# Output copies that read with a stride and write in sequence, decay tables over two queues, and a new fixed order of the opening, in a fused attention and MLP kernel

## The chip, the cores and the metric

The kernel runs on one core of one Trainium2 chip. The metric is the time of one execution on the device, in microseconds (us). A kernel is called faster or slower only if the difference is over 2%.

The engines are written PE (TensorE, matmuls), PEld (its weight loads), DVE (VectorE), ACT (ScalarE), POOL (GpSimd) and SP (SyncE, which here only starts transfers). A profile's span is about 1.75 us shorter than the time of the same execution (222.3 us and 224.09 before). Each execution also comes with the mean clock that was granted to TensorE, as a share of full speed.

## The reference, cut to what matters

The kernel computes a block-wise linear attention with decay, followed by an MLP with a periodic activation. There are 4 batches, 8 heads, 768 tokens and head size 64.

```python
def _attn_ref(q, k, v, lam):                    # cut
    for b in range(nb):                         # blocks of 64 tokens
        intra = einsum('bhic,bhjc->bhij', qb, kb) * Dmask      # lam ** (i - j), causal
        intra = einsum('bhij,bhjd->bhid', intra, vb)
        inter = einsum('bhid,bhde->bhie', qb * lam_pow, kv_state)
        out[:, :, sl] = intra + inter
        kv_state = lam_block * kv_state + einsum('bhsd,bhse->bhde', kb * rev_pow, vb)

def _moe_ref(x, w_in, w_out, alpha):            # x: 3072 x 512, w_in: 512 x 2048, w_out: 2048 x 512
    h = x @ w_in
    s = np.sin(alpha * h)
    g = h + s * s / (alpha + 1e-09)
    return g @ w_out
```

## The kernel before

The kernel works in blocks of 128 tokens, so attention has 24 steps (six for each batch). Four steps make one chunk of 512 tokens for the MLP, and there are six chunks. For each chunk the MLP has 16 "A" groups (w_in, then sine on ACT, square on POOL, DVE or ACT, and the sum `gT` on DVE) and 16 "B" groups (w_out). PE has by far the most work (busy 209.8 of 222.3 us; DVE 152.1, ACT 139.2), so the question is always when PE has to wait.

All operations are recorded first. A small list scheduler in the program then places them in an order for each engine, by assumed durations. Three strings or tables steer it: `LOADS` (the order of the transfers that SP starts), `SCRIPT` (the order of the work on PE) and, after the change only, `ENG` (operations that must run on a given engine). The item `w1` in `SCRIPT` is a filler: a matmul on zeros whose result nobody reads, there to keep PE busy.

For the first steps, q is loaded in rows of 1 KB (four tokens of 64 values), not of 256 bytes. The tokens of such a block arrive permuted: what lies at `g * 4 + t` in order lies at `t * 32 + g` here. The permutation is undone where the attention output is copied from PSUM into `xT`, the MLP's input:

```python
            x_out, x_in = xT[x][:, :, col:col + 128], dst      # dst: PSUM, fp32; xT: SBUF, bf16
            if s < NPQ:                                        # NPQ = 10: the permuted steps
                x_in = dst.rearrange("p a (t g) -> p a t g", g=32)
                x_out = bass.AP(xT[x], col, [[NKC * TCH, 128], [TCH, NKC], [1, 4], [4, 32]])
            rec((("ACT", 0.59), ("DVE", 0.66)), lambda e, name: copy_of(e, name, x_out, x_in), ...)
```

This reads PSUM in sequence and writes bf16 with a step of four elements (8 bytes). The decay tables come from `lam` in two small transfers, both started by ACT. The table `Lk` scales k, and the table `L4` scales permuted q:

```python
            rec("ACT", lambda e: e.dma_start(lam_bc[:, :], ...), 0.5, writes=["lam"], prio=-1)
            ...                                                # lnlam, lnL, Lq
            rec("ACT", lambda e: e.activation(Lk[:, :, :], lnL[:, :, :], ACTF.Exp, scale=-1.0), 0.3,
                reads=["lnL"], writes=["Lk"])
            rec("ACT", lambda e: e.dma_start(lam4_sb[:, :], lam4), 0.5, writes=["lam4"], prio=-2)
            rec("ACT", lambda e: e.activation(lnlam4[:, :], lam4_sb[:, :], ACTF.Ln), 0.3,
                reads=["lam4", "table"], writes=["lnlam4"], prio=-1)
            ...                                                # L4
```

A lower `prio` goes first on its engine, so `lam4` is started before `lam_bc`. The profile leaves numbers out of names: what it calls `lam_sb` is `lam4_sb`.

## Time and profile before

| | time, us | span, us | granted clock |
|---|---|---|---|
| three timed runs | 221.70, 221.84, 222.15 (median 221.84) | not listed | not listed |
| the profiled run | 224.09 | 222.3 | 0.985 |

The page of the kernel before, its head and three rows of the table of 40 slices (5.6 us each; a digit is a share in tenths, 9 is 90% or more):

```profile
span 222.3 us, 3797 instructions
...
PE   7586899899999999999999999999999999999994
...
PEclk9889699999999999999999999999999999999999
DMA  5999999999999899999899998440002110011123
```

PE is busy from the ninth slice on. The clock is below full in slices 2, 3 and 5, with a low of 0.6 in the fifth (22 to 28 us). The DMA engines are nearly full until about 140 us (8 or 9 in the slices from 5.6 us on).

The clock's row tells nothing of the first microseconds. Its record begins at 6.07 us here, and what comes before is counted as full speed. The weight loads of the fillers at the start are 0.43 us apart, though, where matmuls of the same width later start 0.216 us apart:

```profile
3.73 0.15 PEld L773 LDWEIGHTS m_ps<-zeros,ident 128*128 128x128 bf16 x1 [0.28 <-issue]
4.16 0.15 PEld L773 LDWEIGHTS m_ps<-zeros,ident 128*128 128x128 bf16 x1 [0.28 <-issue]
```

"Full clock" and "no stretch" below mean after this opening.

The same by windows:

```profile
core 0: us, PE busy (x) PEld busy (x) DVE busy (x) ACT busy (x) POOL busy (x), PEclk, DMA share, GB/s
...
24.00:28.00 4.00, 4.00 (x19) 1.72 (x19) 1.67 (x4) 1.50 (x4) 0.00 (x0) 0.68 1.17 298
...
36.00:44.00 8.00, 6.94 (x50) 3.01 (x48) 7.66 (x12) 7.71 (x14) 6.02 (x7) 1.00 1.05 341
...
60.00:200.00 140.00, 140.00 (x991) 67.33 (x991) 106.21 (x158) 97.11 (x161) 44.67 (x45) 1.00 0.68 135
```

From 60 to 200 us PE has no gap at all. What can be won lies before 60 us. In 24 to 28 us PE is busy throughout, but at a granted clock of 0.68. In 36 to 44 us it stands idle for 1.06 us.

The timeline of the opening (start, duration, engine, line, what; in brackets the idle time before it and what ended it). The first MLP group is the last line:

```profile
6.28 0.24 ACT L492 ACTIVATE Lk<-lnL 128x48 f32<-128x48 f32 x1 [0.27 <-DVE lnL L488]
...
19.94 1.29 ACT L550 CAST xT<-m_ps 128x512 bf16<-128x512 f32 x1 [0.36 <-PE m_ps L656]
...
21.25 0.37 ACT L550 CAST Zs<-Z_ps 64x256 bf16<-64x256 f32 x1
...
21.67 0.40 PE L652 MATMUL m_ps<-qkT,Zs 128*128 128x128 bf16 x4 [1.32 <-ACT Zs L550]
22.45 1.30 ACT L550 CAST xT<-m_ps 128x512 bf16<-128x512 f32 x1 [0.84 <-PE m_ps L656]
...
23.90 1.86 PE L701 MATMUL m_ps<-xT,w 128*128 128x512 bf16 x4 [1.04 <-ACT xT L550]
```

The copy of 1.29 us at 19.94 holds ACT until 21.23. Only then does ACT copy the attention state `Zs` that step 3 waits for, and step 3's own copy of 1.30 us stands directly before the first group. The group's four matmuls take 1.86 us. In the groups of instructions of the first 60 us, such a copy is:

```profile
L550 ACT CAST xT<-m_ps 128x512 bf16<-128x512 f32 x7 | 9.1, 1302 | 8.7 <-PE m_ps L656 8.7
```

### The profile page before, as it was taken

Reading aid. Unit: us, or ns where it says so; the run is one execution under the profiler, and the core shown is the slowest. Engines: PE = TensorE matmul, PEld = TensorE weight load, DVE = VectorE, ACT = ScalarE, POOL = GpSimd, SP = SyncE. Lnnn points to the kernel's source line nnn. Section 1 sums busy time; section 2 is a strip of 40 time slices with the busy share of each in tenths; the row PEclk is TensorE's granted clock in tenths of the full one; section 3 lists DMA queues with packets and bytes.
Section 4 is the critical chain, followed back from the end, with each engine's and each line's share of the span. In section 5 each row is a group of like instructions: output and inputs, shape, how many; then the busy total and the mean of one; then the engine's idle time right before and its main releaser. Section 6 shows DMA issues by size and latency. Waiting matters only on the chain.

```text
span 222.3 us, 3797 instructions
## 1 busy us (share of the span) xinstructions
PE 209.8 (94%) x1512; PEld 102.6 (46%) x1512; DVE 152.1 (68%) x227; ACT 139.2 (63%) x226; POOL 69.6 (31%) x79
## 2 busy tenths in 40 slices
PE   7586899899999999999999999999999999999994
PEld 2354344445445554444445445444454444444453
DVE  3786589996569997488887947698581788751010
ACT  3458599943888885678974356897655676640111
POOL 4251099740058921254745422311000011000000
PEclk9889699999999999999999999999999999999999
DMA  5999999999999899999899998440002110011123
GB/s 112 283 230 324 302 326 350 330 325 255 225 253 166 152 220 189 270 214 250 173 198 228 231 195 186 129 50 1 0 3 94 47 47 3 0 47 47 47 97 142
DMA packets 92322, 37.49 MB, mean 169 GB/s; under 512 B 80384, under 2 KB 87312, under 8 KB 92304
## 3 DMA queue, kind: packets, MB, share of 16 engines
q1 hardware_dynamic: 88528, 31.07, 65.3%
q10 hardware_dynamic: 3776, 6.18, 8.0%
q8 instruction: 12, 0.20, 0.4%
q14 instruction: 6, 0.05, 0.1%
HBM read 27.28 MB, written 6.29 MB: 151 GB/s over the span
## 4 chain that ended last, share of the span: by engine, by line
PE 84%; DVE 7%; ACT 4%; DMA 2%; issue 0%; SPq 0%; DVEq 0%
PE m_ps L701 36%; PE m_ps L732 35%; PE A_ps L630 3%; ACT xT L550 3%; DMA k<-in_k_dram 2%; DVE S_m L634 2%; PE m_ps L656 2%; PE m_ps L754 2%; PE A_ps L656 1%; PE m_ps L652 1%; DVE gT L716 1%; DVE qk L578 1%; DVE u L713 1%; PE m_ps L609 1%; PE Z_ps L676 1%; PE A_ps L652 1%
## 5 line engine op out<-in xcount | busy, mean ns | idle before, releaser
L701 PE MATMUL m_ps<-xT,w 128*128 128x512 bf16 x384 | 92.9, 383 | 2.3 <-ACT xT L550 1.4
L732 PE MATMUL m_ps<-w,gT 128*128 128x512 bf16 x368 | 87.2, 379 | 0.0
L707 ACT ACTIVATE t<-m_ps,alpha_sb 128x512 bf16<-128x512 f32 x96 | 64.9, 687 | 32.3 <-PE m_ps L701 31.6
L716 DVE SCALAR_TENSOR_TENSOR gT<-u,r_sb,m_ps 128x512 bf16<-128x512 bf16 x96 | 69.2, 741 | 9.8 <-POOL u L713 6.0
L713 POOL TENSOR_TENSOR u<-t 128x512 bf16<-128x512 bf16 x26 | 27.8, 1074 | 92.3 <-ACT t L707 92.1
L701 PEld LDWEIGHTS m_ps<-xT,w 128*128 128x128 bf16 x384 | 35.8, 98 | 45.1 <-issue 2.7
L732 PEld LDWEIGHTS m_ps<-w,gT 128*128 128x128 bf16 x368 | 34.7, 98 | 40.7 <-issue 0.7
L713 DVE TENSOR_TENSOR u<-t 128x512 bf16<-128x512 bf16 x36 | 18.4, 512 | 20.7 <-ACT t L707 20.7
L550 ACT COPY osb<-m_ps 128x512 f32<-128x512 f32 x18 | 10.6, 586 | 21.3 <-PE m_ps L732 21.2
L712 ACT ACTIVATE u<-t 128x512 bf16<-128x512 bf16 x34 | 21.3, 629 | 0.8
L550 ACT CAST xT<-m_ps 128x512 bf16<-128x512 f32 x14 | 13.9, 995 | 12.5 <-PE m_ps L656 12.5
L572 POOL TENSOR_TENSOR qk<-k,Lk 128x512 bf16<-128x512 f32 x16 | 18.1, 1137 | 11.3 <-DMA k<-in_k_dram 7.3
L634 DVE TENSOR_TENSOR S_m<-A_ps,mask 128x1024 bf16<-128x1024 f32 x14 | 17.1, 1220 | 2.1 <-PE A_ps L630 2.0
L550 DVE COPY osb<-m_ps 128x512 f32<-128x512 f32 x5 | 3.4, 689 | 17.1 <-DMA out_dram<-osb 14.5
L634 DVE TENSOR_TENSOR S_m<-A_ps,maskP 128x1024 bf16<-128x1024 f32 x10 | 12.2, 1220 | 1.8 <-PE A_ps L630 1.7
L550 DVE CAST Zs<-Z_ps 64x256 bf16<-64x256 f32 x17 | 7.1, 419 | 6.7 <-PE Z_ps L676 6.5
L581 POOL TENSOR_TENSOR qk<-q,Lq 128x512 bf16<-128x512 f32 x9 | 10.1, 1119 | 3.9 <-DMA q<-in_q_dram 3.8
L630 PE MATMUL A_ps<-qkT 64*128 64x128 bf16 x192 | 9.8, 222 | 1.4 <-DVE S_m L634 1.3
L773 PE MATMUL m_ps<-zeros,ident 128*128 128x512 bf16 x23 | 9.4, 528 | 1.6 <-POOL ident L514 1.6
L550 ACT CAST v<-v 128x512 bf16<-128x512 f32 x15 | 9.3, 622 | 2.2 <-DMA v<-in_v_dram 2.2
L630 PEld LDWEIGHTS A_ps<-qkT 64*128 64x128 bf16 x192 | 5.6, 95 | 9.8 <-issue 3.9
L550 ACT CAST Zs<-Z_ps 64x256 bf16<-64x256 f32 x23 | 8.6, 374 | 0.2
(71 smaller groups left out, 130.5 us busy)
## 6 DMA issues: line engine op xcount, KB each, us to landing
k<-in_k_dram SPq DMA_DIRECT2D x24, 256.0 KB, 5.3
q<-in_q_dram SPq DMA_DIRECT2D x24, 256.0 KB, 5.1
v<-in_v_dram SPq DMA_DIRECT2D x24, 256.0 KB, 5.1
out_dram<-osb ACTq DMA_DIRECT2D x23, 256.0 KB, 2.1
wst<-in_moe_w_in_dram SPq DMA_DIRECT2D x8, 512.0 KB, 7.0
wst<-in_moe_w_out_dram SPq DMA_DIRECT2D x8, 512.0 KB, 5.7
qkT<-qk SPq DMA_TRANSPOSE x14, 3.9
out_dram<-osb ACTq DMA_DIRECT2D x1, 128.0 KB, 1.7
```

What stands on the lines that cost most here:

```text
L550: return e.copy(out_ap, in_ap) if name == "ACT" else e.tensor_copy(out_ap, in_ap)
L572: rec(two, lambda e, _: e.tensor_tensor(k2[c], k32[r][:, :, :], Lk_b, ALU.mult), reads=[f"k32.{r}", "Lk"], writes=[f"k2.{c}"], tag=f"k{s}")
L581: rec(two, lambda e, _: e.tensor_tensor(q2[c], q32[r][:, :, :], Lq_b, ALU.mult), reads=[f"q32.{r}", "Lq"], writes=[f"q2.{c}"], tag=f"q{s}")
L630: last = e.matmul(A_ps[:, 4 * h + jp, :], qkT[j][rows, 4 + jp, :], qT(s, rows, jp))
L634: rec("DVE", lambda e: e.tensor_tensor(S_m[j2][:, :, :], A_ps[:, :, :], mask_b, ALU.mult), 1.22, reads=["S0", "S1", "maskP" if s < NPQ els ...
L701: last = e.matmul(m_ps[i][:, 0:n], w1[:, kc, 128 * m:128 * (m + 1)], xT[x][:, kc, 0:n], start=(kc == 0), stop=(kc == NKC - 1))
L707: rec("ACT", lambda e: e.activation(t16[tt][:, 0:n], m_ps[i][:, 0:n], ACTF.Sin, scale=alpha_sb[:, m:m + 1]), 0.27 + 0.41 * f, reads=[f"m.{ ...
L712: return e.activation(u16[tt][:, 0:n], t16[tt][:, 0:n], ACTF.Square)
L713: return e.tensor_tensor(u16[tt][:, 0:n], t16[tt][:, 0:n], t16[tt][:, 0:n], ALU.mult)
L716: rec("DVE", lambda e: e.scalar_tensor_tensor(out=gT[g][:, m, 0:n], in0=u16[tt][:, 0:n], scalar=r_sb[:, m:m + 1], in1=m_ps[i][:, 0:n], op0 ...
L732: last = e.matmul(m_ps[bank][:, :], gT[g][:, m, 128 * s4:128 * (s4 + 1)], w2[:, m, :], start=(m == 0), stop=(m == NM - 1))
L773: last = e.matmul(m_ps[bank][:, :], ident[:, :], zeros[:, :])
```

## The change

The intent is to shorten the opening. The copies into `xT` are turned round: they read PSUM with a stride and write in sequence. The two `lam` transfers are started by two engines. The order of loads and matmuls and the engines of 56 operations were found by a search. One step fewer is permuted (`NPQ` 9). The penalty in the scheduler's model is an assumption of the program. The middle of the long strings and tables is cut.

```diff
-    "k0 k1 k2 q0 q1 v0 q2 k3 q3 k4 v1 v2 v3 w0 q4 w1 w2 q5 k5 w3 v4 w4 w5 w6 q6 k6 w7 ...
+    "k0 q0 v0 k1 q1 k2 q2 k3 q3 v1 v2 q4 v3 w0 k4 w1 q5 w2 w3 w4 w5 k5 w6 w7 w8 w9 v4 ...
-    "t0 w1 t1 w1 S0 a t2 w1 S1 o0 t3 w1 S2 o1 S3 w1 w1 o2 w1 o3 w1 A0.0 w1 A0.1 T4 A0.2 ...
+    "T0 w1 w1 w1 S0 t1 w1 w1 w1 a w1 S1 t2 w1 o0 S2 t3 w1 o1 S3 w1 o2 w1 w1 w1 o3 A0.0 ...
-NPQ, NW, FETCH = 10, 5, 1.2
+NPQ, NW, FETCH = 9, 5, 1.2
+ENG = {"k0": "DVE", "k1": "DVE", "k2": "POOL", ..., "zs8.1": "ACT"}
@@ in the scheduler: a fixed engine is taken from ENG; its model of time
@@ has a queue for POOL's transfers and a penalty where DVE and POOL overlap
-            rec("POOL", lambda e: e.memset(zeros[:, :], 0.0), 0.5, writes=["zeros"])
+            rec("DVE", lambda e: e.memset(zeros[:, :], 0.0), 0.3, writes=["zeros"], prio=-1)
-                rec("ACT", lambda e: e.dma_start(lam4_sb[:, :], lam4), 0.5,
+                rec("POOL", lambda e: e.dma_start(lam4_sb[:, :], lam4), 0.8,
                     writes=["lam4"], slot="lam4", work=0.05, prio=-2)
             if s < NPQ:
-                x_in = dst.rearrange("p a (t g) -> p a t g", g=32)
-                x_out = bass.AP(xT[x], col, [[NKC * TCH, 128], [TCH, NKC], [1, 4], [4, 32]])
+                x_in = dst.rearrange("p a (t g) -> p a g t", g=32)
+                x_out = x_out.rearrange("p a (g t) -> p a g t", t=4)
```

## The prediction

> **What bounds the kernel now.** By windows, TensorE (PE) is busy without a gap from 60 to 200 us, and that work is fixed. What can be won lies before 60 us. (a) The first MLP group starts at 23.9 us (timeline). (b) It runs its first 2.5 us at half speed: matmuls of 512 columns start 430 ns apart, later 216; the granted clock in 24 to 28 us is 0.68. (c) PE stands idle 1.06 us in 36-44 and 0.47 us in 44-60. The end (2.8 us after PE's last matmul) is not touched.
>
> The opening's chain: tables (Lk ready at 6.5 us, though k0 landed at 3.9), key and query scaling on VectorE (DVE), first transposes at 9.4, four masks of 1.22 us, copies into xT on ScalarE (ACT). Copies of permuted steps take 1.30 us, those of later steps 0.58 (ACT) or 0.69 (DVE), same shape. They delay ACT directly: the state copy that attention step 3 waits for stood behind xT's copy until 21.25.
>
> A second limit lies close: the load queue. DMA share is 0.99 or more per window from 8 to 150 us; loads land one after another, 1.1 to 1.2 us each for k, q, v and 1.5 to 2 us per weight block. The last weight block landed at 52.2 us, v7 (needed for the second chunk) at 53.4; the second chunk's first matmul began at 59.9.
>
> **What the change does.**
> - xT copies: written in sequence, read from PSUM with stride. I expect about 0.6 us on ACT, 0.7 on DVE: 0.6 to 0.7 saved on each of 9. No such strided PSUM read is in the trace. [...]
> - Two lam loads in parallel: lam_bc goes first on ACT and should land near 4.1 instead of 5.8 us, so key scaling starts near 5. [...]
> - q0 and v0 come right after k0: first transposes near 7, not 9.4.
> - Fixed engines, new order: balance only.
>
> **How much counts.** The order still brings v3 13th and w0 14th: by the old landings v3 near 17.4, w0 near 19.1. After its cast (1.1 us) the first group can start near 20.3: 3.6 us earlier. But weight blocks then come at about PE's pace, so part returns as waits for weights; v7 keeps landing near 54, so the second chunk can't start before about 55.5. I expect 56 to 57, with one left-over block of chunk 0 behind it, not two. Net gain about 3.8 us: 221.84 to **218.1 us**, range 216.4 to 219.8. Faster by over 2%: 0.32; within 2%: 0.67; slower: 0.01.
>
> **To check.** Permuted xT copies 0.55 to 0.75 us; Lk by 5.2; first transposes at 6.6 to 7.6; first group at 19.8 to 21.3; second chunk at 55.5 to 57.5; DMA still full; no gaps from 60 us on.
>
> **What would make it wrong.** Strided PSUM reads as slow as the strided writes (then 219 to 220); the half-speed stretch falling elsewhere (1.7 us either way); loads flowing faster once buffers come free sooner (then 216); new waits past 60 us from the new order.

## The result, and the profile after

Ratios in this document are the mean time of one kernel's fast runs over that of the other's fast runs of the same rounds, so they are not quite the ratio of the medians quoted beside them. "Fast" runs are those within 1.5% of the fastest of the same kernel.

| | median, us | all runs, us |
|---|---|---|
| before | 221.77 | 221.32, 221.70, 221.84, 222.15 |
| after | 220.43 | 220.25, 220.36, 220.49, 220.64 |

The ratio is 0.9941 (95% interval 0.992 to 0.9962), which is "same" at 2%. The gain is 1.3 us, where 3.7 us had been forecast (221.84 to 218.1). The measured time lies outside the forecast range of 216.4 to 219.8.

The page after. The profiled execution took 220.64 us, at a granted clock of 1.0:

```profile
span 218.9 us, 3772 instructions
...
PE   5786997999999999999999999999999999999995
...
PEclk9999999999999999999999999999999999999999
DMA  4999999999999999998999999241101110012023
```

```profile
core 0: us, PE busy (x) PEld busy (x) DVE busy (x) ACT busy (x) POOL busy (x), PEclk, DMA share, GB/s
...
24.00:28.00 4.00, 3.87 (x28) 1.74 (x26) 3.60 (x6) 3.48 (x7) 2.08 (x2) 1.00 1.11 344
...
36.00:44.00 8.00, 5.99 (x51) 2.93 (x51) 6.46 (x9) 5.87 (x10) 5.53 (x7) 1.00 1.07 337
...
60.00:200.00 140.00, 138.05 (x963) 66.72 (x980) 103.23 (x155) 95.93 (x162) 33.73 (x34) 1.00 0.68 139
```

The spans of the two profiles differ by 3.4 us (222.3 and 218.9), close to what was forecast. The times of the two kernels differ by 1.3 us. Both are right: the two executions of before that one compares with are not alike. The half speed is gone from the profile after. The last window must be read with care. It holds 963 matmuls but 980 weight loads, where before had 991 of each, so 17 matmul records are missing from the trace (25 of the 752 large matmuls in the whole run). At about 0.2 us each they can account for the 1.95 us that PE seems to stand idle.

The timeline of the opening after, with the same events:

```profile
6.10 0.20 ACT L576 ACTIVATE lnlam<-lam_sb 128x2 f32<-128x2 f32 x1 [1.94 <-DMA lam_sb<-in_lam_dram]
6.40 0.52 ACT L579 ACTIVATE L<-E_f,lnlam 128x24 f32<-128x24 f32 x2
6.82 0.23 ACT L561 ACTIVATE Lk<-lnL 128x48 f32<-128x48 f32 x1
...
20.54 1.04 POOL L619 CAST w<-wst 128x1024 bf16<-128x1024 f32 x1 [2.64 <-DMA wst<-in_moe_w_in_dram]
20.67 0.58 ACT L619 CAST xT<-m_ps 128x512 bf16<-128x512 f32 x1 [1.16 <-PE m_ps L725]
...
21.63 1.04 PE L770 MATMUL m_ps<-xT,w 128*128 128x512 bf16 x4 [0.88 <-POOL w L619]
```

The copy takes 0.58 us. The first group starts 2.27 us earlier, and its four matmuls take 1.04 us where they took 1.86. What it waits for has changed: `xT` is ready at 21.25, but the first weight block only lands at 20.48 and is cast until 21.58. `Lk` comes no earlier: it ends at 7.05 us, where it had ended at 6.52. ACT's fixed order puts the tables of `lam_sb` before it, and `lam_sb` lands last.

The groups of the first 60 us: the copies after the change, on both engines.

```profile
L619 DVE CAST xT<-m_ps 128x512 bf16<-128x512 f32 x3 | 2.1, 688 | 0.1
...
L619 ACT CAST xT<-m_ps 128x512 bf16<-128x512 f32 x3 | 1.8, 585 | 3.1 <-PE m_ps L725 3.1
```

The chain of waits after, for 27 to 40 us (start, length, what):

```profile
27.05 8.23 DMA wst<-in_moe_w_in_dram
...
35.33 1.04 POOL w L619
36.37 1.01 POOL u L782
...
37.40 2.08 DVE gT L785 x3
39.48 0.59 PE m_ps L801 x2
```

A weight block lands at 35.27. POOL casts it, and only then squares one group's sine, and DVE builds three `gT` behind that. PE waits for them twice, 1.62 and 0.23 us. This is a new wait, and it begins with a transfer. It is where part of the earlier start is given back: idle time in 36 to 44 us rose from 1.06 to 2.01 us (0.16 us of it, at 42.2 us, may be a missing record).

### The profile page after: what moved, and what is told of

It is laid out like the page before. It is cut to its first block, busy times and chain, and to the rows that moved or that the text cites. A ratio compares the mean times of both kernels' runs of the same rounds, so it can differ in the third digit from the quotient of the medians.

```text
span 218.9 us, 3772 instructions
## 1 busy us (share of the span) xinstructions
PE 204.8 (94%) x1483; PEld 101.4 (46%) x1510; DVE 148.9 (68%) x227; ACT 136.5 (62%) x232; POOL 63.0 (29%) x73
## 4 chain that ended last, share of the span: by engine, by line
PE 81%; DMA 7%; SPq 6%; DVE 2%; issue 2%; POOL 1%
PE m_ps L801 37%; PE m_ps L770 33%; DMA wst<-in_moe_w_in_dram 7%; SPq L543 6%; PE A_ps L699 3%; PE A_ps L725 2%; PE m_ps L823 2%; DVE gT L785 2%; PE m_ps L725 1%; PE A_ps L721 1%; POOL w L619 1%; PE Z_ps L745 1%; PE m_ps L721 1%; POOL u L782 0%; PE A_ps L681 0%
## 5 line engine op out<-in xcount | busy, mean ns | idle before, releaser
L770 PE MATMUL m_ps<-xT,w 128*128 128x512 bf16 x369 | 90.0, 379 | 4.3 <-DVE gT L785 1.8
L781 ACT ACTIVATE u<-t 128x512 bf16<-128x512 bf16 x45 | 28.1, 629 | 1.2
L703 DVE TENSOR_TENSOR S_m<-A_ps,mask 128x1024 bf16<-128x1024 f32 x15 | 18.3, 1222 | 6.4 <-PE A_ps L699 6.1
L782 POOL TENSOR_TENSOR u<-t 128x512 bf16<-128x512 bf16 x11 | 11.4, 1039 | 25.1 <-ACT t L776 25.1
L641 POOL TENSOR_TENSOR qk<-k,Lk 128x512 bf16<-128x512 f32 x11 | 12.2, 1111 | 16.7 <-DMA k<-in_k_dram 14.3
L650 POOL TENSOR_TENSOR qk<-q,Lq 128x512 bf16<-128x512 f32 x11 | 13.2, 1203 | 9.1 <-DMA q<-in_q_dram 8.8
L641 DVE TENSOR_TENSOR qk<-k,Lk 128x512 bf16<-128x512 f32 x13 | 10.5, 810 | 3.5 <-ACT Lk L561 2.7
L619 ACT CAST Zs<-Z_ps 64x256 bf16<-64x256 f32 x27 | 9.8, 365 | 4.5 <-PE Z_ps L745 2.9
L647 POOL TENSOR_TENSOR qk<-q,L 128x512 bf16<-128x512 f32 x8 | 8.8, 1111 | 9.4 <-DMA q<-in_q_dram 6.0
L619 POOL CAST w<-wst 128x1024 bf16<-128x1024 f32 x9 | 9.3, 1038 | 7.5 <-DMA wst<-in_moe_w_in_dram 7.5
```

Source lines behind the costliest of these rows:

```text
L619: return e.copy(out_ap, in_ap) if name == "ACT" else e.tensor_copy(out_ap, in_ap)
L641: rec(two, lambda e, _: e.tensor_tensor(k2[c], k32[r][:, :, :], Lk_b, ALU.mult), reads=[f"k32.{r}", "Lk"], writes=[f"k2.{c}"], tag=f"k{s}")
L650: rec(two, lambda e, _: e.tensor_tensor(q2[c], q32[r][:, :, :], Lq_b, ALU.mult), reads=[f"q32.{r}", "Lq"], writes=[f"q2.{c}"], tag=f"q{s}")
L703: rec("DVE", lambda e: e.tensor_tensor(S_m[j2][:, :, :], A_ps[:, :, :], mask_b, ALU.mult), 1.22, reads=["S0", "S1", "maskP" if s < NPQ els ...
L770: last = e.matmul(m_ps[i][:, 0:n], w1[:, kc, 128 * m:128 * (m + 1)], xT[x][:, kc, 0:n], start=(kc == 0), stop=(kc == NKC - 1))
L781: return e.activation(u16[tt][:, 0:n], t16[tt][:, 0:n], ACTF.Square)
```

## The experiments

Two theories were set against each other at the start. The first says that the strided-read copies carry the gain, and that the tables and the search add nothing. The second says that every part contributes, and that the gain is lost later, at the load queue. A third question, why the profiles showed 3.4 us and the times 1.3, was put to runs as well.

Eighteen runs were made, some of one kernel twice, each beside runs of the kernel before on the same chip. Unless a run is said to be wrong, its result agreed with the reference.

### The copies alone, the rest alone, and before once more

`x_only` is the kernel before with the copies' new form and nothing else. `x_undo` is the kernel after with the copies' old form. Together they split the change in two.

```diff
 # x_only, on the kernel before                     # x_undo is the reverse, on the kernel after
-                x_in = dst.rearrange("p a (t g) -> p a t g", g=32)
-                x_out = bass.AP(xT[x], col, [[NKC * TCH, 128], [TCH, NKC], [1, 4], [4, 32]])
+                x_in = dst.rearrange("p a (t g) -> p a g t", g=32)
+                x_out = x_out.rearrange("p a (g t) -> p a g t", t=4)
```

`before_again` has no edit.

> The kernel before, unchanged, to see whether its first profile stands for its timed runs. Theory A: the half-speed stretch at 23 to 27 us (granted clock 0.985 over the span) belonged to that one profiled execution (224.1 us); the timed runs (221.3 to 222.2) did not have it. Then spans here are about 220.0 us at clock 1.00 for most runs, and the first MLP group runs its matmuls 216 ns apart from the start. Rival B: every run has the stretch; then clock 0.985 in each and spans near 222.

> The kernel before with the strided-read copies into xT alone; order of all engines the same. Theory (copies stand on the chain to the first group): copies fall from 1.30 to about 0.6 us, the state copy before step 3 no longer waits, first group about 1.5 to 2.5 us earlier than in the kernel before, time down by 1 to 2 us. Rival (loads bind): copies fall, but the time falls by less than 0.7 us, since the weight blocks land when they did.

> The kernel after with strided writes into xT again, same order. If the copies carry the gain: 1 us or more slower than after, that is back at the kernel before or worse (ratio 1.000 or above). If the order carries it: ratio stays near 0.995.

| same chip | median, us | runs, us | ratio to before (95%) |
|---|---|---|---|
| before, 8 runs | 223.78 | 221.14 to 226.26 | |
| before_again, 2 runs | 224.17 | 222.62, 225.72 | 1.0107 (0.9928 to 1.0287) |
| x_only | 220.41 | 219.76 to 220.75 | 0.9928 (0.9873 to 0.9983) |
| x_undo | 221.82 | 221.54 to 222.08 | 1.0001 (0.9961 to 1.0041) |

The copies alone gain as much as the whole change. The rest alone gains nothing against the fast runs of before. That ratio leaves out four of the eight runs of before, the slower ones, and the section on the clock below comes back to them.

The groups of `x_undo`, first 60 us, show that DVE suffers from strided writes as ACT does, so that the copies' cost belongs to the form and not to the engine (the strided reads took 585 ns on ACT and 688 on DVE in the groups above; in the later steps of before, copies that read and write in sequence take 584 and 691):

```profile
L619 DVE CAST xT<-m_ps 128x512 bf16<-128x512 f32 x3 | 3.9, 1303 | 0.1
L619 ACT CAST xT<-m_ps 128x512 bf16<-128x512 f32 x3 | 3.9, 1302 | 2.2 <-PE m_ps L725 2.2
```

`x_only` did what its theory said in time (1.5 us at full clock, see below), but its first group came only 1.2 us earlier (22.71 us), not 1.5 to 2.5. Neither expectation of `before_again` held: its profiled run had the half speed at the first group again (0.985, 225.72 us), its other run less of it (0.992), and one of the eight runs beside it had none.

The unexpected finding is the width of before: 5 us between its fastest and slowest run on one chip (eight runs), where `x_only` spreads over 1.0 and `x_undo` over 0.5 (four runs each).

### The tables, one queue or two, and cheap loads

`lam_undo` is the kernel after with both `lam` transfers started by ACT, `lam_sb` first, as before. `lam_early` keeps one queue too, but starts `lam_bc` first and makes `Lk` before the tables of `lam_sb`. In both, `q0` is pinned to POOL so that all other orders stay as they are after the change. `cheap_kv` is the kernel after with k and v of the first nine steps loaded in 1 KB rows too. Its tokens are then in the wrong places and its result is wrong (relative error 0.81). It asks what the load queue costs. (In the profile of before, the q loads in 1 KB rows that landed at 8.95, 11.14 and 13.06 us came 0.83 to 0.89 us after the load ahead of them, and the k and v loads at 12.23, 14.26, 15.48 and 16.66 us 1.08 to 1.21 us.)

```diff
 # lam_undo, on the kernel after
-                rec("POOL", lambda e: e.dma_start(lam4_sb[:, :], lam4), 0.8,
+                rec("ACT", lambda e: e.dma_start(lam4_sb[:, :], lam4), 0.5,
 # lam_early: the same, and
-                    writes=["lam4"], slot="lam4", work=0.05, prio=-2)
+                    writes=["lam4"], slot="lam4", work=0.05, prio=-1)
-                reads=["lnL"], writes=["Lk"])
+                reads=["lnL"], writes=["Lk"], prio=-2)
-                    reads=["lam4", "table"], writes=["lnlam4"], prio=-1)
+                    reads=["lam4", "table", "Lk"], writes=["lnlam4"], prio=-1)
 # cheap_kv, on the kernel after, for k and v
+                if s < NPQ:
+                    a = bass.AP(src.tensor, ..., [[4 * D, 32], [2 * S * D, 4], [S * D, 2], [1, 4 * D]])
+                    d = bass.AP(dst[r], 0, [[H * D, 128], [4 * D, 2], [1, 4 * D]])
```

> The kernel after with both lam loads on ScalarE's queue again, the per-step table first as in the kernel before; nothing else moves but three small instructions. Theory (in the kernel after the table path got worse, Lk at 7.05 against 6.52, because its second load from GpSimd landed at 6.1 us and ScalarE's order puts Lk behind it, but it binds nothing): Lk near 6.5, first transposes about 0.5 us earlier, first group within 0.3 us of 21.6, time within 0.3 us of after. Rival (the opening's chain from the tables binds): 0.5 us faster than after.

> Both lam loads on ScalarE's queue, lam_bc first, and Lk made before the other table. Lk should be ready near 4.7 us instead of 7.05, the other table near 6. First transposes then wait for q0 (lands at 6.8) and come near 8.0 instead of 8.8. Theory (loads bind the first group): it still starts at 21.3 to 21.7, time within 0.4 us of after. Rival (tables bind): first group 0.8 us or more earlier, time near 219.6.

> Wrong result on purpose: k and v of the first 9 steps are fetched in rows of 1 KB as q is, same bytes and same buffers but the wrong tokens, so each of these loads should take about 0.8 instead of 1.2 us. Order of all engines as in after. Theory (the load queue binds the opening): w0 lands about 2.5 to 3 us earlier, w15 and v7 about 5 us earlier, first group near 20 us (then the attention chain binds), waits for weights at 36 to 39 us go, time 1.5 to 3 us below after. Rival (chains on the engines bind): time within 0.5 us of after.

| same chip | median, us | Lk ends | first group of chunk 0 | first group of chunk 1 |
|---|---|---|---|---|
| lam_undo | 220.11 | 8.22 | 21.76 | 56.58 |
| lam_early | 220.06 | 4.28 | 21.46 | 56.96 |
| cheap_kv | 217.90 | | 22.23 | 56.09 |

In this table and those below, the start of chunk 1 is that of its first weight load; its first matmul follows within 0.22 us. The timelines of `lam_undo` and, below it, of `lam_early`:

```profile
4.39 0.20 ACT L577 ACTIVATE lnlam<-lam_sb 128x2 f32<-128x2 f32 x1 [1.08 <-DMA lam_sb<-in_lam_dram]
...
7.98 0.24 ACT L562 ACTIVATE Lk<-lnL 128x48 f32<-128x48 f32 x1 [1.11 <-DVE lnL L558]
```

```profile
4.04 0.24 ACT L562 ACTIVATE Lk<-lnL 128x48 f32<-128x48 f32 x1 [0.27 <-DVE lnL L558]
5.81 0.20 ACT L577 ACTIVATE lnlam<-lam_sb 128x2 f32<-128x2 f32 x1 [1.40 <-DMA lam_sb<-in_lam_dram]
```

The order of ACT's work moves `Lk` by 3.9 us and the time by 0.05 us. (`lam_undo` was expected to bring `Lk` near 6.5; it came at 8.22, since `lam_bc` landed at 6.63 us, where it had landed at 5.77 in before, and DVE then took 1.05 us for `lnL`, not 0.21.) One transfer's table comes early and the other's late in either case, and the first transposes need both. In the order after the change, the tables are not what bounds.

The later of the two `lam` transfers landed at 5.77 us (before, both on ACT), 6.08 (after, on POOL), 5.79 (`lam_early`, both on ACT) and 6.63 us (`lam_undo`, both on ACT). The second queue brought no gain here. (`lam_sb` is the later one after the change and in `lam_early`, `lam_bc` in the other two.)

Cheaper loads gained 2.2 us against `lam_undo`, although the first group started 0.5 us later and not near 20 us, as had been expected. The last weight block landed at 47.79 us, where it landed at 52.19 in `lam_undo` and at 53.27 in the profile after. So in the order after the change, the stream of loads does bind. (k, v and weights all land earlier in this run, so it does not tell them apart.) The windows say where, first `lam_undo` and then `cheap_kv`, with the columns of the windows shown before:

```profile
20.00:44.00 24.00, 22.26 (x158) 10.59 (x158) 20.21 (x31) 19.34 (x32) 15.23 (x16) 1.00 1.11 342
```

```profile
20.00:44.00 24.00, 23.03 (x164) 11.02 (x163) 21.32 (x32) 19.50 (x33) 16.28 (x15) 1.00 1.01 343
```

PE is busy 0.77 us longer in these 24 us. That is a part of the 2.2 us. The rest was not traced to single waits.

### The clock

The profile of before has two stretches at half speed after the opening, 9.48 to 12.89 and 23.13 to 26.55 us, 3.413 us each, with a granted clock of 0.50 throughout. The second lies on the first MLP group. `before_warm` has 6 fillers where before has 1, in the two places ahead of the first group, to see whether they keep that stretch away. `before_p2` and `before_p3` are before unedited, to see more profiles of it. `x_cold` is `x_only` with four fillers cut to 16 columns, so that PE is less busy there (its expectation says five; the edit and the trace have four).

```diff
 # before_warm, on the kernel before; the scheduler is still told of one
-    ... S3 w1 w1 o2 w1 o3 w1 A0.0 ...
+    ... S3 w1 w1 o2 w6 o3 w6 A0.0 ...
 # x_cold, on x_only; an f1 is a filler of 16 columns
-    ... S3 w1 w1 o2 w1 o3 w1 A0.0 ...
+    ... S3 f1 f1 o2 f1 o3 f1 A0.0 ...
```

> The kernel before with 10 more warm-up matmuls in the idle time of TensorE before the first group (6 instead of 1 in two places), order otherwise the same. Theory (the kernel before is slow in some runs, 223 to 226 us, because TensorE's clock was halved for 3.4 us from about 23 us on after the idle time at 20.5 to 23.9): no half-speed stretch at the first group, all runs at 221 to 221.8 us, and the first group's start unchanged at 23.8 to 24.0. Rival (the spread has another cause): runs of 223 us and more appear as before.

> The kernel before once more, for one more profile. Theory (its slow runs of 223 us and more have TensorE's clock halved for one 3.4 us window at the first group; its runs below 222.5 do not): if this execution is above 223 us, two half-speed windows, the second near 23 us; if below 222.6, no window there. Rival: the time and the window don't go together.

> As before_p2, another execution of the kernel before; the same test of time against window.

> The kernel before with strided-read copies (as x_only) and the five filler matmuls before the first group cut to 16 columns, so that TensorE does 1 us less in 18.7 to 22.7 us; orders unchanged. Theory: the half-speed window at the first group comes back in many runs, as in the kernel before, and those runs are 1.5 to 2.5 us longer than x_only's 219.7 to 220.8; the first group's start stays at 22.6. Rival (the window costs nothing): time as x_only in all runs.

| | median or time, us | half-speed stretches in the profile, us |
|---|---|---|
| before_warm | 222.49 (221.82 to 223.94) | 10.12 to 13.53 |
| before_p2 | 223.48, one run | 11.52 to 18.35 |
| before_p3 | 224.19, one run | 9.81 to 13.22, 23.46 to 26.87 |
| x_cold | 221.95 (219.87 to 223.32) | 11.16 to 17.99, 21.40 to 24.81 |

The ratio of `before_warm` to before is 0.9974 (0.9916 to 1.0032), that of `x_cold` 0.9883 (0.9788 to 0.9977). `before_p3` came out as expected. `before_p2` did not: it is above 223 us and has twice 3.41 us of half speed, but none near 23 us. `before_warm` missed too: all its runs lie above 221.8 us, and its first group started at 23.38 us and not at 23.8 to 24.0.

By themselves these ratios decide nothing. What tells more is the granted clock of every single execution. One stretch of 3.413 us at half speed lowers the mean over 221 us by 0.5 x 3.413 / 221 = 0.0077. So I count 0.992 as one such stretch, 0.985 as two, and 0.977 as three. For runs without a profile this is an estimate; the profiles bear it out (`x_only` 0.992 with one, before 0.985 with two, `x_cold` 0.977 with three, two of them in one stretch of twice the length). The 44 runs of before that stood beside other runs, on five chips, sort like this (the two of `before_again`, `before_p2` and `before_p3` are not counted: one had one stretch and three had two):

| half-speed stretches (granted clock) | before: runs, median us | after: runs, median us | x_only | x_early (below) |
|---|---|---|---|---|
| none (0.998 to 1.0) | 7, 221.73 | 11, 220.25 | 4, 220.25 | 5, 219.68 |
| one (0.991, 0.992) | 16, 223.06 | 5, 221.31 | 6, 219.76 | 5, 219.75 |
| two (0.983 to 0.985) | 13, 224.33 | none | none | none |
| three (0.977) | 8, 224.04 | none | none | none |

Four of the 11 runs of after in the first row are those of the first result. That is the answer to the third question. Before runs in several states of the clock, and its median rises by about 1.3 us with each of the first two stretches. The order none, one, two holds within each of the five chips too, as far as the states occurred, with steps of 0.9 to 2.2 us between medians of one to five runs. Single runs overlap: 220.85 to 222.45 us with none, 221.32 to 223.93 with one, 222.95 to 225.27 with two. Six runs of the last two rows are slow by the rule of 1.5%; without them their medians are 224.21 and 224.01. The profile that the prediction read is a run with two. At two stretches against none, before and after differ by 224.33 - 220.25 = 4.1 us, about what was forecast. At none against none they differ by 1.5 us, which is about what the first result showed. The clock of those first timed runs of before was not listed, so that they had no stretch or at most one is inferred from their times: none took over 222.15 us, and no run of before with two or three took less than 222.95.

`x_cold` comes from the other side. Its four runs had one, two, three and three stretches, and took 219.87, 221.78, 222.11 and 223.32 us. Its kernel differs from `x_only` only in the width of four fillers. In windows of 20 to 26 us, first `x_only` and then `x_cold`:

```profile
20.00:26.00 6.00, 5.10 (x59) 2.84 (x57) 4.04 (x8) 3.72 (x7) 0.96 (x2) 1.00 1.10 321
```

```profile
20.00:26.00 6.00, 4.44 (x48) 2.63 (x44) 2.91 (x7) 2.61 (x6) 0.27 (x1) 0.72 1.12 315
```

and their first groups in the timeline, in the same order:

```profile
22.71 1.04 PE L701 MATMUL m_ps<-xT,w 128*128 128x512 bf16 x4 [0.23 <-ACT xT L550]
```

```profile
23.30 1.49 PE L701 MATMUL m_ps<-xT,w 128*128 128x512 bf16 x3 [0.74 <-ACT xT L550]
```

The records of three matmuls span 1.49 us where those of four spanned 1.04. The record of the group's first matmul is missing; its weight load started at 22.90 us.

Where a stretch falls seems to matter. `x_only` and `x_early` lose nothing that shows to their one stretch (219.76 us with one and 220.25 with none, 219.75 and 219.68), which in their profiles lies at 9.2 to 13.1 us, before PE has MLP work; the fastest run of `lam_undo` (219.57 us) had one at 8.69 to 12.10. But two in a row there do cost: `before_p2` had both before the first group, which then started at 24.54 us instead of 23.90, and took 223.48 us. `before_warm` kept the stretch off the first group in its profile, and its three runs with one (221.82 to 222.97) have a median 0.6 us below that of before's three on the same chip (222.01 and 222.65), which is little for so few runs. But its fourth run had three stretches and took 223.94 us, so more fillers in these two places are no full cure.

What sets off a stretch was not shown; two profiles can only be set side by side. Before, PE was busy for 0.97 us of the 3.41 us ahead of the first stretch (6.07 to 9.48) and for 1.81 us of those ahead of the second (19.72 to 23.13). In between, it was busy for 2.55 us in 12.89 to 16.30 and for 2.57 us in 16.30 to 19.72, and the clock was 1.00 from 12.89 to 23.13. After the change, whose order has more fillers early on, PE was busy for 2.51 us in 6.07 to 9.48 (2.06 us of it with fillers, 0.93 before) and for 2.46 us in 19.72 to 23.13, where its first group starts, and no stretch came. So in these two profiles the stretches followed the less busy times, and `x_cold` with its narrower fillers had more of them than `x_only`. That is too little for a rule.

### Both kernels again, and attempts at a better order

`after_again` and `after_3` are the kernel after, unedited, and `x_only_2` is `x_only` once more. `best2` is `lam_early` with one square of chunk 0 moved from POOL to DVE (and the others pinned where they were), against the wait found at 36 to 40 us. `best3` also moves a v cast to POOL and three weight casts.

```diff
 # best2, on lam_early
+    "sq0.9": "DVE",
 # best3, on best2
-    "v2": "DVE",
+    "v2": "POOL",
+    "wc7": "POOL", "wc13": "DVE", "wc14": "DVE",
```

> The kernel after, unchanged, beside the kernel before on another chip. Theory (the kernel before is bimodal: 221.1 to 222.4 us or 223 to 226 us, the latter with TensorE's clock halved at the first group, and the kernel after is not): after stays at 220 to 221 us in all runs; the kernel before spreads over 3 us or more; ratio near 0.985 where most runs of before are slow. Rival (the first measurement, ratio 0.994, holds on every chip): ratio 0.992 to 0.996.

> The kernel before with the strided-read copies alone, now beside the kernel after on one chip. Theory (the copies are the whole gain; order and tables add nothing): equal to after_again within 0.4 us. Rival (order and tables add to it): 1 us or more slower than after_again.

> The kernel after with early tables (as lam_early) and the square of block A0.9 moved from GpSimd, where it stood behind the weight cast that waits for w7, to VectorE. Theory (that square's place in GpSimd's queue made VectorE and then TensorE wait, 1.6 us in one wait at 36 to 38 us): TensorE's wait for gT at 36 to 39 us falls below 0.5 us, 0.5 to 1 us below lam_early, 1 us below after_again. Rival (w7 itself binds): the wait remains, time within 0.4 us of after_again.

> As best2, and the cast of v2 on GpSimd instead of VectorE, where it stood in front of the fourth mask. Theory: fourth mask about 0.6 us earlier, xT of step 3 ready near 20.7, first group then bound by w0's cast at 20.6 to 21: first group 0.5 us earlier than lam_early; time 0.3 to 0.6 us below best2. Rival (weights bind what follows): first group earlier, time as best2.

| same chip | median, us | ratio to before (95%) | first group of chunk 0 | of chunk 1 |
|---|---|---|---|---|
| before, 11 runs | 223.93 | | | |
| after_again | 220.52 | 0.9872 (0.982 to 0.9924) | 21.86 | |
| x_only_2 | 219.77 | 0.9838 (0.9787 to 0.9889) | 22.64 | 55.40 |
| best2 | 220.18 | 0.9845 (0.9799 to 0.9892) | 21.47 | 56.80 |
| best3 | 221.97 | 0.9931 (0.9885 to 0.9977) | 20.80 | 58.89 |

On one chip, in the same rounds, the copies alone in the old order are 0.8 us faster than the whole change (means of all runs 219.91 and 220.69). Two of the six runs of `after_again` had a stretch at half speed (221.31 and 221.85 us). Without them its mean is 220.25 and the difference 0.3 us. Either way the searched order does not add to the copies. Neither expectation of `x_only_2` (equal, or 1 us slower) held. `after_again` was not at 220 to 221 us in all runs, and before is spread over its states rather than split in two; but the ratio, 0.9872 here and 0.9911 on a third chip (`after_3` below), shows that the first 0.9941 does not hold wherever before runs with stretches.

`best2` removed the wait it was aimed at. The wait for `gT` fell to 0.2 us, but waits for weight casts of 0.4 and 0.4 us came in its place, and the time hardly moved: 0.3 us below `after_again`, where 1 us had been expected. `best3` has the earliest first group of all kernels and is the slowest of this table but for before, 1.8 us above `best2` where 0.3 to 0.6 us below had been expected. What PE waits for in 20 to 45 us (waiting line, what released it: us in total, times, longest):

```profile
PE m_ps L790 <- DVE gT L805: 1.4, 1, 1.4
PE m_ps L821 <- DVE gT L805: 1.1, 1, 1.1
```

So the start of the first group is a bad measure of the opening. What counts is when chunk 1 can start and how much of chunk 0 is left then.

### The old order with early tables

If the order costs and the copies pay, the best version is before with the new copies. `x_early` adds the early `Lk` to it: `lam_bc` first, then `Lk`, all on ACT's one queue. `x_early_2` is the same kernel on another chip, beside `after_3`. `x_early_cheap` gives it k and v in 1 KB rows for the first ten steps (wrong, relative error 0.86), to ask what loads cost in this order.

```diff
 # x_early, on x_only
-                reads=["lnL"], writes=["Lk"])
+                reads=["lnL"], writes=["Lk"], prio=-2)
-                    writes=["lam4"], slot="lam4", work=0.05, prio=-2)
+                    writes=["lam4"], slot="lam4", work=0.05, prio=-1)
-                    reads=["lam4", "table"], writes=["lnlam4"], prio=-1)
+                    reads=["lam4", "table", "Lk"], writes=["lnlam4"], prio=-1)
```

> As x_only, with lam_bc loaded first and Lk made first on ScalarE's one queue: Lk near 4.5 instead of 6.8 us. Theory (tables bind nothing, loads of q0 and the chain of masks do): time within 0.4 us of x_only, 219.5 to 220.4. Rival: 0.5 us or more faster, which would beat all kernels so far.

> The old order with strided-read copies and early tables, beside the kernel after on one chip. Theory (the new order and engine table lose about what the earlier start wins): 0.5 to 1 us below after_3, at 219.5 to 219.8 with a spread below 0.5 us. Rival (the difference seen so far is between chips): equal within 0.3 us.

> The kernel after, on the chip of x_early_2. 220 to 221 us if the theory holds, with a spread of 1 to 2 us.

> Wrong result on purpose: x_early with k and v of the first 10 steps fetched in 1 KB rows, same bytes, buffers and order. Theory (the load queue, not the opening's chain, binds the better order too): the weights land several us earlier, time 1.5 to 2.5 us below x_early_2. Rival (TensorE's own work binds by now): within 0.5 us.

| | median, us | ratio to before (95%) | first group of chunk 0 | of chunk 1 |
|---|---|---|---|---|
| x_early (first chip) | 219.63 (219.57 to 219.75) | 0.983 (0.9778 to 0.9881) | 21.53 | 55.38 |
| x_early_2 (second chip) | 219.86 (219.63 to 220.56) | 0.9873 (0.9819 to 0.9926) | 20.92 | 55.67 |
| after_3 (second chip) | 220.64 (220.04 to 221.95) | 0.9911 (0.9858 to 0.9963) | 22.38 | 57.07 |
| x_early_cheap (second chip) | 219.50 (219.31 to 220.80) | 0.9868 (0.9817 to 0.9918) | 21.20 | 55.11 |

`x_early` beats both kernels. Its mean is 0.8 us below that of `after_3` on the same chip (219.94 and 220.77), with five lines of the source of before changed. Against the three runs of `after_3` at full clock (mean 220.15) the lead is 0.2 us; the rest of it comes from the other three, which had a stretch at half speed. (`x_early_2` had one in three of its six runs too, and spread over 0.9 us, not the 0.5 expected.) The timeline of `x_early`, tables and first group:

```profile
4.22 0.24 ACT L492 ACTIVATE Lk<-lnL 128x48 f32<-128x48 f32 x1 [0.28 <-DVE lnL L488]
...
21.53 1.04 PE L701 MATMUL m_ps<-xT,w 128*128 128x512 bf16 x4 [0.24 <-ACT xT L550]
```

The early table brings the first group forward by 1.1 us against `x_only_2`, but chunk 1 starts at 55.4 in both (at 56.37 in the profile of `x_only` itself). It is worth little or nothing more than `x_only`: the two never ran on one chip.

Cheap loads gain only 0.4 us in this order, against 2.2 in the order after the change, although v7 lands at 47.59 us. So the load queue does not bind the old order. In 21 to 55 us of `x_early_cheap`, PE is nearly full, and its largest waits are spread over state copies (0.6 us), a weight cast on DVE (0.6) and transposes (0.5). The limits there are nearly equal, which is why one of them alone moves little.

## Why the prediction was wrong, point by point

The forecast was "same" as the likelier outcome, and that held. The time was 2.3 us too low, and outside the range.

1. **The sum's start: the step that failed.** "Net gain about 3.8 us: 221.84 to 218.1 us." The 3.8 us were read from a trace whose own execution took 224.09 us at a clock of 0.985, and were taken off a median of 221.84 from other executions. The two profiles do differ by 3.4 us. So the sum itself was mis-sized by little. But "it runs its first 2.5 us at half speed" was a property of that execution's state and not of the kernel in every run: three of the four profiles of before have it, and the timed runs of the baseline, by their times, had at most one stretch. What failed is the subtraction of a gain read in one state from a time taken in another. At equal states, runs of before without half speed differ from runs of after by 1.5 us, and that is what the sum should have held for this baseline. Taken off the 224.09 us of its own execution, the same 3.8 us would have given 220.3. The prediction named this risk ("the half-speed stretch falling elsewhere, 1.7 us either way") but did not look which state its baseline was in.
2. **Copies: right.** "0.55 to 0.75 us" was forecast and 0.585 us on ACT and 0.69 on DVE were measured. `x_only` shows that they carry the gain: at full clock, 221.73 us of before become 220.25 with the copies alone and 221.82 with the rest alone (`x_undo`).
3. **Tables: wrong in direction.** "Lk by 5.2" was forecast and 7.05 was measured. The prediction looked at when `lam_bc` would land (it did land early: its logarithm starts at 3.96) and not at ACT's order, which puts the tables of `lam_sb` before `Lk`. It also expected the transfers to run "in parallel". The start on POOL held it for 0.77 us (1.25 to 2.02). The first transposes came at 8.80, not at 6.6 to 7.6. It did not matter: `lam_early` mended it and gained nothing over `lam_undo`, where `Lk` came later still.
4. **First group: nearly.** 19.8 to 21.3 was forecast and 21.63 was measured (21.86 and 22.38 in two more profiles), since the first weight block landed at 20.48 and not near 19.1.
5. **Chunk 1: nearly.** 55.5 to 57.5 was forecast and 57.67 was measured; v7 landed at 54.31 ("near 54"), and one block of chunk 0 was left over, as forecast. The new wait at 36 to 40 us, behind a weight block, is the "waits for weights" that was expected.
6. **New order: mis-sized.** "Balance only" was booked as zero. Against the copies in the old order it costs 0.8 us over all runs of one chip (`x_only_2` against `after_again`), and 0.3 us where runs with a stretch at half speed are left out. What it does bring is a steadier clock: its part alone (`x_undo`) ran at full clock in four of four runs and the whole change in 11 of 16, where before did so in 7 of 44 (with the copies alone, 4 of 10, and none with two stretches). I take this to be its fillers, a guess from the opening (2.06 us of fillers after and 0.93 before in 6.07 to 9.48, as above), but no run has those fillers alone in the old order.
7. **DMA full, no gaps past 60 us: right.** Apart from missing records, PE is full from 60 to 200 us in both. The DMA share is 1.02 or more in every window from 8 to 100 us, and 0.89 in 100 to 150 us (before: 1.00).

What stays open is how much a single stretch costs before by its place, since no run of before with none, with one or with three was profiled, and where a half-speed stretch falls when it costs the kernel after 1.1 us (221.31 and 220.25), since none of those runs was profiled. Nor is it shown which single wait makes up all of the 2.2 us that loads cost in the order after.

## What to carry to other kernels

Before subtracting a gain from a time, check that the trace and the time belong to the same state: compare the profiled run's own time and clock with the timed runs (here 224.09 us at 0.985, beside 221.70 to 222.15 us). When a layout has to be undone in a copy from PSUM to bf16 in SBUF, measure both directions, since here the strided read cost nothing (585 and 688 ns on ACT and DVE, against 584 and 691 in sequence) and the strided write about doubled the copy (1302 and 1303). An earlier first matmul is no gain by itself. Follow the work to where PE stays full, and try the one good line in the old order before trusting a searched new one.
